# A fused attention and feed-forward kernel: chunks 3 and 4 turned by VectorE, and new lists that set the order of the work

## Chip, cores and metric

One core of a Trainium2 chip runs the whole kernel. The metric is device time in microseconds of one execution, the median of several runs; less is better. The profile is one further execution with the hardware profiler. TensorE's granted clock is at its upper level (2.4 GHz) throughout: the page shows 9 in each of 40 slices, 90% or more of it.

## What is computed

Attention with pooled keys and values for 8 batches and 8 heads (576 queries, head size 64, keys and values averaged over 8 neighbours to 72), then a feed-forward layer with softplus over all 4608 tokens (512 wide, 2048 hidden):

```python
k_p = k.reshape(B, H, Sp, pool, D).mean(axis=3)          # Sp = 72
v_p = v.reshape(B, H, Sp, pool, D).mean(axis=3)
scores = scale * np.matmul(q, k_p.transpose(0, 1, 3, 2))
scores = scores - np.max(scores, axis=-1, keepdims=True)
attn = np.exp(scores)
attn = attn / (np.sum(attn, axis=-1, keepdims=True) + 1e-09)
x = np.matmul(attn, v_p)                                  # to (4608, 512)
h = x @ w_in
g = np.maximum(h, 0.0) + np.log1p(np.exp(-np.abs(h)))
out = g @ w_out
```

All is float32. Large products are made of three products of rounded parts: each operand is split into a rounded value in the type fp32r and a remainder (`x` is both parts of the attention's output, `w` and `l` those of the weights, `gh`/`g` and `gl` those of the softplus).

## The kernel before

The 4608 tokens are cut in 18 chunks of 256 (`CT`), each of two tiles of 128 tokens (`T`). For each chunk come the attention (queries against the 72 pooled keys, exponential, probabilities times values, which gives `x`) and the feed-forward layer (`h` from `x`, `g` from `h`, and the product with the second weight). The program has two parts.

The **first part** holds the feed-forward work of chunks 0 to 2 (`feed`; lines 690 and 715), the attention of chunks 0 to 3 (`attend`), the making of the split weights from the integer halves that are loaded, and the pooling of keys and values. The **steady part** holds the feed-forward work of chunks 3 to 17, in pairs of two pieces of the hidden width (`first_products`, line 743, then `second_products`), each beside the attention of the next chunk. Chunk 3's second products are 24 straightforward ones (`pair2`, line 786); from chunk 4 on (`NF` = 4) a pair is made of seven products of combined operands (line 895). For these VectorE and ScalarE make sums of pieces of `g` (`sf`, `so`: lines 805 to 824), and, once, combinations of weights (`d`, `t`, `w`: lines 848 to 864).

The attention needs its queries and its probabilities with tokens along the free axis. Two ways to turn them exist:

- By TensorE: products with an identity matrix. Queries: `qT`, line 403, names `qTp<-ident,q`. Probabilities of the first 64 keys: `PT`, line 484, `ptp<-ident,pm`. Those of the last 8 keys, in three copies: lines 496 and 610, `ltp<-ident,pe`. ScalarE copies each result out of PSUM. Chunks 0 to 2 do so, chunk 3 (in `attend(N1)`, `N1` = 3, tile by tile) and chunk 4 (`BY_PE = (4,)`).
- By VectorE, chunks 5 to 17: a stream transpose of blocks of 32 by 32 (`turn`, line 524, 128x1024 elements). For queries ScalarE then spreads the blocks by 16 copies (line 535). For probabilities four stores (`leave`, line 528) and one load (`enter`, line 531) on SyncE's queue carry the blocks through memory. The last keys are turned on VectorE too (line 1487), and spread by 12 small copies.

After that come the scores (lines 423 and 557), the smallest negated score and its subtraction (`least`, `less`), one exponential for a chunk, sums and reciprocal, the products `pm` and `pe`, and the product with the values (`avp`, lines 657 and 664); ScalarE rounds it (`x`, line 671) and VectorE makes the remainder (line 674).

What stands in a row on each engine is not the order of the code. Each step is entered as an operation with an engine, a cost, what it comes after, and the buffers (slots) that it uses. A planner (`Order.run`) lays the operations out one after another: of those that could begin first it takes the one of highest rank, which is the length of the longest chain that follows it plus a number `first`. Two tables written by hand, `HASTE` for the first part and `SOONER` for the steady part, add to `first` of single operations by their number. The order found is emitted as it stands, so an engine that reaches an instruction whose input is late stands still with all that is behind it.

## Time and profile before

| what | us |
|---|---|
| median of 3 runs | 862.92 |
| lowest and highest | 862.19 and 863.48 |
| span of the profiled execution | 860.2 |
| TensorE busy | 847.5 (99%) |
| TensorE loading weights | 823.3 (96%) |
| VectorE busy | 666.3 (77%) |
| ScalarE busy | 509.2 (59%) |

The span runs from the first to the last instruction on the core; the device time of the runs also holds what lies around it, and the median is 2.7 us above this span. The page is read from the chain that ended last (which engine sets the end), then by stages, since the engines' shares differ between the first 340 us and the rest, and then by the waits of the engine that the chain names.

### The profile page before, as it was taken

To read this page: it belongs to the slowest core of one execution; us is meant where nothing else is said; L and a number is where in the kernel's file an instruction comes from. 1 tells how busy PE (TensorE), PEld (TensorE's weight loads), DVE (VectorE), ACT (ScalarE), POOL (GpSimd) and SP (SyncE) were. 2 spreads that over 40 slices of the span, in tenths; PEclk is the share of its full clock that TensorE was granted. 3 is DMA by queue.
4 is the path that set the end of the run, shared out by engine and by line. 5 is a ranking of instruction groups with operands and counts; after the bars stand their busy time and mean duration, and the time that the engine had idled before them with its cause. 6 is when DMAs were issued, how large, how long until landed. Compare 5 with 4: busy or idle time off the path is not lost.

```text
span 860.2 us, 21310 instructions
## 1 busy us (share of the span) xinstructions
PE 847.5 (99%) x8520; PEld 823.3 (96%) x8520; DVE 666.3 (77%) x1562; ACT 509.2 (59%) x1138; POOL 3.8 (0%) x33
## 2 busy tenths in 40 slices
PE   8999999999999989999999999999999999999997
PEld 6799999999999989999999999999999999999997
DVE  6899999868887888877788787877777765667554
ACT  5964333446557785857486837574747676454522
POOL 1000000000000000000000000000000000000000
PEclk9999999999999999999999999999999999999999
DMA  8975536455889789778978897678777666667671
GB/s 261 322 226 177 204 139 196 142 178 182 278 304 287 246 277 290 253 247 272 284 244 266 264 288 256 221 247 289 256 259 246 227 230 220 220 229 245 229 247 74
DMA packets 116451, 204.82 MB, mean 238 GB/s; under 512 B 47104, under 2 KB 68096, under 8 KB 116352
## 3 DMA queue, kind: packets, MB, share of 16 engines
q1 hardware_dynamic: 116352, 203.46, 72.3%
q8 instruction: 67, 1.10, 0.5%
q14 instruction: 32, 0.26, 0.1%
HBM read 174.06 MB, written 29.36 MB: 236 GB/s over the span
## 4 chain that ended last, share of the span: by engine, by line
PE 92%; DVE 3%; DMA 2%; ACT 2%; issue 1%; SPq 0%; DVEq 0%; ACTq 0%
PE h L743 37%; PE m L895 30%; PE acc L715 7%; PE h L690 6%; PE acc L786 3%; PE avp L657 2%; PE sc L557 2%; PE avp L664 1%; DMA l<-wi 1%; DMA t<-t 1%; DMA kvst<-in_k_dram 1%; PE kps L1134 1%; ACT qT L535 1%; ACT E L448 0%; PE m L557 0%
## 5 line engine op out<-in xcount | busy, mean ns | idle before, releaser
L743 PE MATMUL h<-x,l 128*128 128x256 f32 x2748 | 333.1, 277 | 0.1
L743 PEld LDWEIGHTS h<-x,l 128*128 128x128 f32 x2748 | 321.8, 188 | 0.7 <-DMA l<-wi 0.3
L751 ACT ACTIVATE g<-h 128x512 f32<-128x512 f32 x120 | 71.9, 599 | 159.7 <-PE h L743 156.5
L895 PE MATMUL m<-w,so 128*128 128x256 f32 x1134 | 149.0, 277 | 1.2 <-ACT so L819 1.0
L895 PEld LDWEIGHTS m<-w,so 128*128 128x128 f32 x1134 | 137.9, 188 | 1.8 <-ACT so L819 1.2
L819 ACT CAST so<-sf 128x512 fp32r<-128x512 f32 x112 | 69.7, 622 | 52.8 <-DVE sf L808 50.0
L805 DVE TENSOR_TENSOR sf<-g 128x128 f32<-128x128 f32 x112 | 32.2, 288 | 85.9 <-ACT g L751 85.5
L824 DVE TENSOR_TENSOR so<-sf,so 128x512 fp32r<-128x512 f32 x112 | 77.1, 688 | 25.7 <-ACT so L819 24.7
L535 ACT COPY qT<-turn 32x256 f32<-32x256 f32 x208 | 84.1, 404 | 12.2 <-DVE turn L524 5.0
L895 PE MATMUL m<-w,gh 128*128 128x256 f32 x476 | 90.4, 278 | 0.0
L772 DVE TENSOR_TENSOR gl<-g,gh 128x384 fp32r<-128x384 f32 (+1 forms) x120 | 67.3, 561 | 7.3 <-ACT gh L765 5.2
L895 PEld LDWEIGHTS m<-w,gh 128*128 128x128 f32 x476 | 71.8, 188 | 0.6
L895 PE MATMUL m<-w,gl 128*128 128x256 f32 x238 | 65.9, 277 | 0.0
L695 ACT ACTIVATE g<-h 128x256 fp32r<-128x256 f32 x96 | 32.1, 383 | 55.3 <-PE h L690 32.4
L765 ACT ACTIVATE gh<-h 128x384 fp32r<-128x384 f32 (+1 forms) x120 | 59.2, 493 | 0.2 <-DVE gl L772 0.2
L690 PE MATMUL h<-x,w 128*128 128x256 f32 x396 | 49.9, 278 | 0.1
L690 PEld LDWEIGHTS h<-x,w 128*128 128x128 f32 x396 | 47.1, 188 | 0.6 <-ACT g L695 0.3
L715 PE MATMUL acc<-w,g 128*128 128x256 f32 x264 | 47.0, 279 | 0.0
L895 PEld LDWEIGHTS m<-w,gl 128*128 128x128 f32 x238 | 44.7, 188 | 0.0
L916 DVE TENSOR_TENSOR o<-o,m 128x256 f32<-128x256 f32 x98 | 39.8, 418 | 3.3 <-ACT o L908 0.4
L715 PEld LDWEIGHTS acc<-w,g 128*128 128x128 f32 x264 | 39.9, 188 | 0.1
L895 PE MATMUL m<-l,gh 128*128 128x256 f32 x196 | 37.4, 279 | 0.0
(214 smaller groups left out, 1333.3 us busy)
## 6 DMA issues: line engine op xcount, KB each, us to landing
l<-wi SPq DMA_DIRECT2D x224, 512.0 KB
out_dram<-o SPq DMA_DIRECT2D x36, 256.0 KB
q<-in_q_dram SPq DMA_DIRECT2D x32, 256.0 KB
kst<-in_k_dram SPq DMA_DIRECT2D x24, 288.0 KB
moved_p<-turn SPq DMA_DIRECT2D x52, 128.0 KB
pT<-moved_p SPq DMA_DIRECT2D x13, 512.0 KB
vst<-in_v_dram SPq DMA_DIRECT2D x24, 256.0 KB
stage<-in_moe_w_in_dram SPq DMA_DIRECT2D x22, 256.0 KB
```

The costliest lines, as they stand in the source:

```text
L535: nc.scalar.copy(out=o, in_=x[a * B32:(a + 1) * B32, s].rearrange("p (u m i) -> p u m i", u=T, i=B32))
L690: nc.tensor.matmul(out=ps[:, 0:CT], lhsT=row(w, kc), rhs=x[:, kc], start=first and kc == j == 0, stop=last and kc == KC - 1 and j == 2)
L715: nc.tensor.matmul(out=accs[c][t][:, ns], lhsT=a[:, ts], rhs=w[:, ns], start=f == 0 and n == j == 0, stop=f == FC - 1 and n == 1 and j == ...
L743: nc.tensor.matmul(out=ps[:, k * CT:(k + 1) * CT], lhsT=row(w, kc), rhs=x_[c][i][:, kc], start=first and n == 0, stop=last and n == len(or ...
L751: nc.scalar.activation(out=g, in_=x.rearrange("p (b i) -> p b i", i=P), func=AF.Softplus)
L765: nc.scalar.activation(out=gh, in_=quarters(c, x.rearrange("p (b i) -> p b i", i=P)), func=AF.Softplus)
L772: nc.vector.tensor_tensor(out=gl, in0=quarters(c, g), in1=gh.bitcast(F32), op=ALU.subtract)
L805: tt(out=sf[:, 2], in0=g[:, 0], in1=g[:, 2], op=ALU.add)
L819: nc.scalar.copy(out=so[:, 0], in_=ss[c, u])
L824: nc.vector.tensor_tensor(out=so[:, 1], in0=sf, in1=so[:, 0].bitcast(F32), op=ALU.subtract)
L895: nc.tensor.matmul(out=ms[c][n], lhsT=x, rhs=y, start=u == 0 and j == 0 and n in (1, 6, 5, 4), stop=u == FP - 1 and j == 2 and n in (2, 7, ...
L916: nc.vector.tensor_tensor(out=o, in0=in0, in1=m[n], op=how)
```

## The change

Chunks 3 and 4 are turned by VectorE as chunks 5 to 17 are. One function, `turned_attention`, makes the attention of chunks 3 to 17; for chunk 3 (`early`) it is called in the first part, and `attend` is left with chunks 0 to 2. TensorE's transposes of chunks 3 and 4 go: 16 products `qTp`, 16 `ptp` and 6 `ltp`. VectorE gets two turns of 128x1024 and one of 128x128 for each of the two chunks, ScalarE 28 small copies for each, and SyncE's queue four stores and one load of probabilities for each.

The planner of the first part gets what that of the steady part had: a transfer is an operation that holds the queue for a time, and one that holds a resource `TRANSFER` and lands 1.85 us after. Costs of operations are smaller by what is now a lag between engines (0.13 to 0.2 us), and two neighbours on VectorE of which one needs the other get a lag of 0.1 us. `HASTE` and `SOONER` are new throughout. With `short`, the last product of a chunk's last keys is cut in two where the chunk holds queries of two batches, so that the one at the end has 64 columns.

```diff
-                        + [x.end + (x.lag if x.engine != o.engine or x.lag > 1 else 0)
+                        + [x.end + (x.lag if x.engine != o.engine or x.lag > 1 else self.same.get(o.engine, 0))
...
-    BY_PE = (4,)
...
+        i, t = sp[-1]
+        short = [*sp[:-1], (i, slice(t.start, t.stop - D)), (i, slice(t.stop - D, t.stop))]
         for r, ps in enumerate(pss):
             for g in range(2):
-                for i, t in sp:
+                for i, t in short if len(sp) > 1 and r == g == 1 and sp[-1][1].start < CT - D else sp:
                     nc.tensor.matmul(out=ps[:, g * CT + t.start:g * CT + t.stop],
...
+    TRANSFER, LANDING, nothing = "transfer", 1.85, lambda: None
+    LAGS = {PE: 0.2, ACT: 0.14, DVE: 0.13, TRANSFER: LANDING}
+    todo.begin, todo.table = {SYNC: 0.8, TRANSFER: 0}, "exp"
+    todo.in_turn, todo.same = (TRANSFER,), {DVE: 0.1}
+
+    def op(engine, cost, fn, after=(), slots=(), **more):
+
+        if engine is not SYNC:
+            return todo.op(engine, cost, fn, after, slots, LAGS[engine], **more)
+        queue, work = cost
+        o = todo.op(SYNC, queue, fn, after, slots, 0, **more)
+        return todo.op(TRANSFER, work, nothing, [o], slots, LANDING, first=more.get("first", 0))
...
-        return 0.14 + 0.00094 * n
+        return 0.03 + 0.0009 * n
 
     def dve1(n):
-        return 0.14 + 0.00054 * n
+        return 0.06 + 0.00053 * n
...
-                if c < N1:
...
-                    def less(x=x, i=i, s=s):
-                        if c not in e_:
-                            new_E(c)
-                        x.less(i, s.tile)
-                    ends.append(op(DVE, 0.46, less, [d, *e_free], [s, s_mn]))
...
-        if c == N1:
-            ex = op(ACT, 1.2, lambda: exponential(e_[c]), subs, table="exp")
         for x, ends, s_E, s_sm, s_pm, s_pe in norms:
-            if c == N1:
-                ends = [op(DVE, 0.75, lambda x=x, n=s_sm: x.sum(n.name), [ex], [s_sm])]
...
+    def turned_attention(c):
+        early = c == N1
+        here = lambda kind: [] if early else [Slot(kind)]
+        soon = lambda run: {} if early else dict(first=EARLY, home=run)
+        s_q, s_E, s_lt = here("q"), here("E"), Slot("lt_")
+        tiles = [Tile(c, t) for t in range(T)]
+
+        def load():
+            load_q(c)
+        o_q = op(SYNC, (1.1, 2.0), load, [q_free[c - 1, i] for i in range(T)] if early else qT_done.get(c - 1, ()), s_q)
+        subs = []
+        qT_done[c], score_done[c], av_done[c], x_done[c] = [], [], [], []
+        sp, s_mn, x_q = spans(c * CT, (c + 1) * CT), Slot("mn"), []
+        s_t, turns, s_qT = Slot("ld"), {}, [Slot("qT") for _ in range(T if early else 1)]
+
+        def turn_q():
+            turns["q"] = one.tile([P, A, T * HP * B32], F32, tag=s_t.name, name="turn")
+            turn(turns["q"], qt_[c].rearrange("p t h d -> p (t h d)"))
+
+        def spread_q(a, pair):
+            for s in pair:
+                across(q_place(slice(0, T))[s * B32:(s + 1) * B32, :, :, a * B32:(a + 1) * B32],
+                       turns["q"], a, s)
+        for x in tiles:
+            x.q = q_place(x.t)
+        o = op(DVE, 1.17, turn_q, [o_q, *entered["q"]], [*s_q, s_t])
+        qT_done[c].append(o)
+        for a in range(A):
+            for pair in ((0, 1), (2, 3)):
+                x_q.append(op(ACT, 0.83, lambda a=a, pair=pair: spread_q(a, pair), [o], [s_t, *s_qT]))
+        entered["q"] = x_q
+        old = c - 2 if c - 2 >= NF else None
+        ss = [Slot("bank"), Slot("bank"),
+              Slot("bank") if early else Slot("acc") if old is None else banks_of[old][3]]
+
+        def third_bank():
+            return bank(ss[2], "sc") if old is None else ms[old]["rest"]
+        p = op(PE, 1.4, lambda: pair_scores(
+            c, tiles, [*(bank(s, "sc") for s in ss[:2]), (third_bank(), old is None)]),
+               [*x_q, *parts_of(sp, k_done if early else k_ready), m_begun.get(old), *([av[c - 1]] if early else [])],
+               [*s_qT, *ss], **soon("m"))
+        score_done[c].append(p)
+        for j in (2, 0, 1):
+            ps = lambda j=j: third_bank() if j == 2 else ss[j].tile
+            o = op(DVE, 0.22 if j == 2 else 0.6,
+                   lambda j=j, ps=ps: pair_least(c, j, ps(), s_mn.name), [p], [ss[j], s_mn],
+                   first=HURRY if j == 2 else 0)
+            for part in range(1 if j == 2 else 3):
+                subs.append(op(DVE, 0.22 if j == 2 else (0.37, 0.21, 0.14)[part],
+                               lambda j=j, ps=ps, part=part: pair_less(c, j, part, ps()),
+                               [o, *(e_free if early else ())],
+                               [ss[j], s_mn, *s_E], first=HURRY if j == 2 else 0))
+        return lambda where: probabilities(c, s_E, s_lt, subs, where)
...
+    def probabilities(c, s_E, s_lt, subs, where):
+
+        early = c == N1
+        soon = lambda run: {} if early else dict(first=EARLY, home=run)
+        s_pT, s_pe, x, s_sm, s_pm, s_t = Slot("pT"), Slot("pe"), {}, Slot("sm"), Slot("ld"), Slot("ld")
+        if early:
+            ex = op(ACT, 1.1, lambda: exponential(e_[c]), subs, table="exp")
+        else:
+            ex = op(ACT, 1.1 + TABLE, lambda: exponential(e_[c]), [*subs, where], s_E)
+            op(ACT, TABLE, lambda: None, [ex], first=5000)
+
...
+        o = op(DVE, 1.28, sums_p, [ex], [*s_E, s_sm])
+        o = op(DVE, 0.4, reciprocals, [o], [s_sm])
+        m = op(DVE, 1.14, main_p, [o], [*s_E, s_sm, s_pm], first=FIRST)
+        e = op(DVE, 0.2, ends_p, [o], [*s_E, s_sm, s_pe])
+        o = op(DVE, 1.17, turn_p, [m], [s_pm, s_t], first=FIRST)
+        ways = [op(SYNC, (0.5, 0.36), lambda a=a: leave(x["turn"], "p", a), [o, *entered["p"]], [s_t], first=FIRST)
+                for a in range(A)]
+        entered["p"] = [op(SYNC, (0.35, 2.1), enter_p, ways, [s_pT], first=FIRST)]
+        lows = [*entered["p"], *last_keys(c, [o, e], lambda: x["pm"], s_pm, s_pe, s_lt)]
+        sp = spans(c * CT, (c + 1) * CT)
+        ss = [Slot("bank"), Slot("bank")]
+        o = op(PE, 1.7 if len(sp) == 1 else 2.1, lambda: av_products(c, [bank(s, "avp") for s in ss]),
+               [*lows, *parts_of(sp, v_done if early else v_ready), *([x_free[0]] if early else [])],
+               [*ss, s_lt, s_pT], **soon("h"))
+        av_done[c].append(o)
+        s_x = [] if early else [Slot("x")]
+        if s_x:
+            x_slot[c] = s_x[0]
+        for r, s in enumerate(ss):
...
-    attend(N1)
+    turned_attention(N1)(None)
...
-    HASTE = {27: -130, 29: -3, 34: -120, 36: -120, 45: 40, 46: 20, 48: -180, 55: -2, 56: -10, 57:
...
+    HASTE = {2: 5889, 4: 7020, 6: 5020, 8: 1140, 10: 1278, 13: -860, 20: 170, 29: 3721, 31: 3711, 33: 3265, 39:
...
-    with tc.manual_schedule(engines={ACT, DVE, PE, SYNC}):
-        for o in todo.run():
-            o.fn()
+        todo.ops[i].first += x
+    ctx.enter_context(tc.manual_schedule(engines={ACT, DVE, PE, SYNC}))
+    for o in todo.run():
+        o.fn()
...
-        if c in BY_PE:
-            s_qT, s_qb = [Slot("qT")], [Slot("bank") for _ in tiles]
-
-            def transposes():
-                for x, s in zip(tiles, s_qb):
-                    x.qT(bank(s, "qTp"))
-            o = op(PE, 0.97, transposes, [o_q, *av_done.get(c - 1, ())], [s_q, *s_qb], first=EARLY, home="m")
-            qT_done[c].append(o)
-            for x, s, n in zip(tiles, s_qb, Q):
-                x_q.append(op(ACT, act(512), lambda x=x, s=s, n=n: x.qT_out(s.tile, n), [o], [s, *s_qT]))
-        else:
-            s_t, turns, s_qT = Slot("ld"), {}, [Slot("qT")]
...
-        if c in BY_PE:
-            for x in tiles:
-                s_sm, s_pm = Slot("sm"), Slot("G")
-                o = op(DVE, 0.785, lambda x=x, n=s_sm: x.sum(n.name), [ex], [s_E, s_sm])
-                o = op(DVE, 0.44, x.reciprocal, [o], [s_sm])
-                m = op(DVE, 0.72, lambda x=x, s=s_pm: x.main(s.name), [o], [s_E, s_sm, s_pm])
-                es.append(op(DVE, 0.255, lambda x=x, s=s_pe: pair_ends(c, x, s.name), [o], [s_E, s_sm, s_pe]))
-                s = Slot("bank")
-                o = op(PE, 0.55, lambda x=x, s=s: x.PT(bank(s, "ptp")), [m], [s, s_pm], first=EARLY, home="h")
-                lows.append(op(ACT, act(512), lambda x=x, s=s: x.PT_out(s.tile), [o], [s, s_pT]))
-        else:
...
-        if c in BY_PE:
-            s_l = Slot("bank")
-            p = op(PE, 0.27, lambda: pair_last(c, bank(s_l, "ltp")), es, [s_l, s_pe], first=EARLY, home="m")
-            for a in range(2):
-                h = op(ACT, act(256), lambda a=a: pair_high(c, a, s_l.tile, a), [p], [s_l, s_lt])
-                lows.append(op(DVE, dve2(256), lambda a=a: pair_low_ends(c, a, s_l.tile), [h], [s_l, s_lt]))
-            for a in range(2):
-                lows.append(op(ACT, act(256), lambda a=a: pair_high(c, a, s_l.tile, 2), [p], [s_l, s_lt]))
-        else:
-            lows += last_keys(c, [o, *es], lambda: x["pm"], s_pm, s_pe, s_lt)
...
-                    rest = steady_attention(c + 1)
+                    rest = turned_attention(c + 1)
...
-    SOONER = {37: -100.0, 43: -300.0, 44: -100.0, 48: -700.0, 49: -900.0, 53: -50.0, 58: -400.0, 59: -400.0,
...
+    SOONER = {17: 1346, 18: 2216, 28: 99, 36: -84, 44: -1517, 50: -21, 51: 527, 69: -2053, 77: -29, 83: -13.8,
```

On TensorE, at the start of the steady part: the end of a row of chunk 3's h products (`h<-x,w`), then chunk 4's queries turned, then chunk 3's second products (`acc<-w,gh` and `acc<-w,gl`). Before:

```order
L743 MATMUL h<-x,w 128x256 x24
L403 MATMUL qTp<-ident,q 128x128 x8
L786 MATMUL acc<-w,gh 128x256 x2
L786 MATMUL acc<-w,gl 128x256
L786 MATMUL acc<-w,gh 128x256 x2
L786 MATMUL acc<-w,gl 128x256
L786 MATMUL acc<-w,gh 128x256 x2
```

After, the same place:

```order
L744 MATMUL h<-x,w 128x256 x24
L787 MATMUL acc<-w,gh 128x256 x2
L787 MATMUL acc<-w,gl 128x256
L787 MATMUL acc<-w,gh 128x256 x2
L787 MATMUL acc<-w,gl 128x256
L787 MATMUL acc<-w,gh 128x256 x2
```

The eight transposes are gone; h and the second products are neighbours.

On TensorE, at the seam of the two parts: chunk 3's product with the values (`avp`), chunk 2's products (`h<-x,l`, `acc<-l,g`), and the first of chunk 3's h (`h<-x,w` at line 743). Before:

```order
L715 MATMUL acc<-l,gl 128x256
L657 MATMUL avp<-pT,vs_102 64x256 x8
L664 MATMUL avp<-lt__1039,vlo_104 128x256 x4
L690 MATMUL h<-x,l 128x256 x48
L715 MATMUL acc<-l,g 128x256 x2
L743 MATMUL h<-x,w 128x256 x17
L715 MATMUL acc<-l,gl 128x256
```

After:

```order
L691 MATMUL h<-x,l 128x256 x12
L656 MATMUL avp<-pT,vs_102 64x256 x8
L665 MATMUL avp<-lt__2440,vlo_104 128x256 x4
L716 MATMUL acc<-l,g 128x256 x2
L716 MATMUL acc<-l,gl 128x256
L716 MATMUL acc<-l,g 128x256 x2
L716 MATMUL acc<-l,gl 128x256
L716 MATMUL acc<-l,g 128x256 x2
L716 MATMUL acc<-l,gl 128x256
L716 MATMUL acc<-l,g 128x256 x2
L716 MATMUL acc<-l,gl 128x256
L744 MATMUL h<-x,w 128x256 x24
```

In the rows before, 48 products of chunk 2 and two more stand between `avp` and chunk 3's h; in those after, twelve do. Chunk 3's scores (`sc`), which stood in one row before some 51 us into the span and a second one later, now stand as one row late in the first part, with 168 products of 256 columns and a small transpose from there to `avp`:

```order
L716 MATMUL acc<-l,g 128x256 x2
L716 MATMUL acc<-l,gl 128x256
L691 MATMUL h<-x,l 128x256 x12
L556 MATMUL sc<-kT_100,qT 64x72 x32
L691 MATMUL h<-x,l 128x256 x12
```

On VectorE, in chunk 4's first combined products: sums of `g` (`sf`, `so`), weights' combinations (`t`, `w`), and the probabilities of the next chunk (`sm`, `pm`). Before:

```order
L805 TENSOR_TENSOR sf<-g 128x128
L806 TENSOR_TENSOR sf<-g 128x128
L807 TENSOR_TENSOR sf<-sf,g 128x128
L808 TENSOR_TENSOR sf<-g,sf 128x128
L772 TENSOR_TENSOR gl<-g,gh 128x384
L864 TENSOR_TENSOR t<-d,t 128x2x256
L824 TENSOR_TENSOR so<-sf,so 128x512
L864 TENSOR_TENSOR w<-d,w 128x2x256 x2
L1529 TENSOR_REDUCE sm<-E 128x16
L1533 TENSOR_SCALAR sm<-sm 128x16
L1534 RECIPROCAL sm<-sm 128x16
```

After, from the same sums on:

```order
L806 TENSOR_TENSOR sf<-g 128x128
L807 TENSOR_TENSOR sf<-g 128x128
L808 TENSOR_TENSOR sf<-sf,g 128x128
L809 TENSOR_TENSOR sf<-g,sf 128x128
L523 STREAM_TRANSPOSE turn<-q 128x8x4x32
L825 TENSOR_TENSOR so<-sf,so 128x512
L253 TENSOR_TENSOR vst<-vst 128x2x256
L253 TENSOR_TENSOR vst<-vst 128x2x128
L253 TENSOR_TENSOR vp<-vst 128x128
L1381 TENSOR_REDUCE sm<-E 128x16
L1385 TENSOR_SCALAR sm<-sm 128x16
L1386 RECIPROCAL sm<-sm 128x16
```

The turn of a chunk's queries and the pooling of values (`vst`, `vp`) stand where the weights' combinations stood. Behind them, where before a second set of sums, `pm` and a turn of probabilities followed, the pooling of keys (`kst`, `kp`) now stands as well:

```order
L809 TENSOR_TENSOR sf<-g,sf 128x128
L773 TENSOR_TENSOR gl<-g,gh 128x384
L825 TENSOR_TENSOR so<-sf,so 128x512
L253 TENSOR_TENSOR kst<-kst 72x2x256
L253 TENSOR_TENSOR kst<-kst 72x2x128
L253 TENSOR_TENSOR kp<-kst 72x128
L773 TENSOR_TENSOR gl<-g,gh 128x384
L523 STREAM_TRANSPOSE turn<-pm 128x8x4x32
```

## Rows read from the trace of the kernel before

**Rows 1.** The page, busy time by engine, and the last chain by engine:

```profile
PE 847.5 (99%) x8520; PEld 823.3 (96%) x8520; DVE 666.3 (77%) x1562; ACT 509.2 (59%) x1138; POOL 3.8 (0%) x33
...
PE 92%; DVE 3%; DMA 2%; ACT 2%; issue 1%; SPq 0%; DVEq 0%; ACTq 0%
```

**Rows 2.** Windows: us; busy us (instructions) PE, PEld, DVE, ACT, POOL; clock; DMA:

```profile
60.00:80.00 20.00, 19.85 (x173) 19.59 (x172) 19.43 (x36) 9.33 (x23) 0.00 (x0) 1.00 0.41 136
160.00:245.00 85.00, 84.45 (x869) 82.91 (x868) 68.83 (x153) 44.86 (x92) 0.21 (x2) 1.00 0.65 213
340.00:600.00 260.00, 259.93 (x2657) 255.14 (x2651) 203.63 (x517) 173.13 (x368) 0.63 (x6) 1.00 0.81 263
600.00:855.00 255.00, 255.00 (x2529) 251.69 (x2528) 167.86 (x434) 141.52 (x294) 0.42 (x4) 1.00 0.67 226
```

**Rows 3.** Waits of TensorE: line, releaser: us in total, times, longest:

```profile
PE acc L715 <- DVE gl L701: 1.0, 2, 0.5
PE m L895 <- ACT so L819: 1.0, 1, 1.0
PE m L557 <- ACT qT L535: 0.9, 1, 0.9
PE avp L657 <- DVE E L595: 0.8, 1, 0.8
...
PE m L895 <- DVE so L824: 0.2, 1, 0.2
```

**Rows 4.** Timeline of TensorE, chunk 4's queries: start, us, instruction:

```profile
185.50 2.88 PE L743 MATMUL h<-x,w 128*128 128x256 f32 x24
188.23 1.04 PE L403 MATMUL qTp<-ident,q 128*128 128x128 f32 x8
189.02 0.48 PE L786 MATMUL acc<-w,gh 128*128 128x256 f32 x2
189.34 0.28 PE L786 MATMUL acc<-w,gl 128*128 128x256 f32 x1
```

**Rows 5.** Timeline of TensorE, chunk 3's probabilities, chunk 4's last keys:

```profile
62.75 0.63 PE L484 MATMUL ptp<-ident,pm 128*128 128x128 f32 x4
63.13 0.48 PE L715 MATMUL acc<-w,g 128*128 128x256 f32 x2
63.46 0.28 PE L715 MATMUL acc<-w,gl 128*128 128x256 f32 x1
...
215.91 0.38 PE L610 MATMUL ltp<-ident,pe 128*64 128x128 f32 x2
216.04 1.17 PE L743 MATMUL h<-x,l 128*128 128x256 f32 x8
```

**Rows 6.** Groups of VectorE by shape: busy us, mean ns | idle before:

```profile
L772 DVE TENSOR_TENSOR gl<-g,gh 128x384 fp32r<-128x384 f32 x112 | 61.8, 552 | 3.0 <-ACT gh L765 3.0
...
L674 DVE TENSOR_TENSOR x<-avp,x 128x512 fp32r<-128x512 f32 x36 | 23.7, 684 | 3.7 <-ACT x L671 3.6
...
L253 DVE TENSOR_TENSOR kst<-kst 72x512 f32<-72x512 f32 x24 | 16.3, 680 | 0.3 <-DMA kst<-in_k_dram 0.3
...
L524 DVE STREAM_TRANSPOSE turn<-q 128x1024 f32<-128x1024 f32 x13 | 16.1, 1237 | 0.0
```

**Rows 7.** Groups of ScalarE by shape, the rounding of x:

```profile
L671 ACT CAST x<-avp 128x512 fp32r<-128x512 f32 x36 | 19.8, 589 | 8.9 <-PE avp L664 8.8
```

**Rows 8.** Waits of VectorE, 160 to 245 us:

```profile
DVE vst L253 <- DMA vst<-in_v_dram: 2.3, 1, 2.3
```

**Rows 9.** Timeline, two turned chunks: scores and turn; turn, reading back, product:

```profile
339.78 1.07 PE L557 MATMUL sc<-kT,qT 64*64 64x72 f32 x53
...
351.98 1.25 DVE L524 STREAM_TRANSPOSE turn<-pm 128x1024 f32<-128x1024 f32 x1
...
486.16 1.25 DVE L524 STREAM_TRANSPOSE turn<-pm 128x1024 f32<-128x1024 f32 x1 [0.65 <-ACT qT L535]
...
491.56 0.32 SPq L531 DMA_DIRECT2D pT<-moved_p  x1
...
499.04 1.09 PE L657 MATMUL avp<-pT,vs 64*64 64x256 f32 x16
```

More of the change, by code (lines that the diff above doesn't have):

```diff
@@ L1191, in attend @@
             ends, ss = [], [Slot("bank"), Slot("bank")]
-            p = op(PE, 0.7, lambda x=x, ss=ss: x.scores([bank(s, "sc") for s in ss]), [o, *keys],
+            p = op(PE, 0.72, lambda x=x, ss=ss: x.scores([bank(s, "sc") for s in ss]), [o, *keys],
                    [s_qT, *ss])
@@ new lines, in pooled_attention_softplus_ffn @@
+    todo.last = Op(None, 0, None, (), (), 0, -1)
+    s_w, x_w = Slot("bank"), []
+    o = op(DVE, 0.3, lambda: x_w.append(ones()), first=2000)
+    op(PE, 3.6, lambda: warm(x_w[0], bank(s_w, "warm"), (512, 384)), [o], [s_w], first=2000)
+    batch(0)
+    batch(1)
+    for f in range(FC):
+        weights(f)
+    for c in range(N1):
+        attend(c)
+    for c in range(N1 - 1):
+        feed(c)
+    todo.first = 1000
+    turned_attention(N1)(None)
+    todo.first = 0
+    feed(N1 - 1)
+    keys_values(2, score_done[N1 - 1], [av[N1 - 1]])
@@ new lines, in pooled_attention_softplus_ffn @@
+    other = [b for b in BANKS if b not in acc_banks]
+    kinds = {"h": other[:2], "acc": other[2:4], "bank": other[4:], "ld": LD, "q": "a", "pT": "a", "qT": "a", "lt_": "a",
+             "pe": "a", "mn": "ab", "sm": "ab", "E": "a", "kp": "a", "vp": "a", "S": "ab", "x": "b",
+             **{y.kind: {"a": "b", "b": "a"}[y.name] for y in last_g},
+             "G": [f"G{i}" for i in range(4)] + O}
+    ends = {e: max(o.end for o in todo.ops if o.engine == e) for e in (ACT, DVE, PE, SYNC, TRANSFER)}
```

372 lines of the change are left out of this document (139 added, 233 removed), and 83 rows, old and new, of tables (HASTE, SOONER).

## The prediction

> **What bounds the kernel now.** I read the page's busy times and its chain first: TensorE is busy for 847.5 us of an 860.2 us span, and 92% of the chain that ended last is TensorE's [rows 1]. So the end moves with what TensorE has to do and with the moments at which it stands idle; nothing that VectorE or ScalarE saves counts by itself. The windows say where that can change: from 340 us to 855 us TensorE is busy for 514.9 of 515 us and VectorE for 371 [rows 2]; nothing there waits, so nothing there can be won by a better order. In 60 to 80 us the picture is another: VectorE is busy for 19.43 of 20 us beside TensorE's 19.85, so the two run in lockstep, and work added to VectorE there is felt at once. In 160 to 245 us VectorE has 16.2 of 85 us free [rows 2], though part of that is waiting: 2.3 us of it is one load of values [rows 8]. The list of TensorE's waits gives the idle time that can vanish: 0.5 us at the first part's end (one of the two waits for gl), then 1.0, 0.2, 0.9 and 0.8 us in the 300 to 322 us stretch, 3.4 us in all [rows 3]. The other 0.5 us for gl lies at 43.8 us, in front of any change, and I let it stand.
>
> The profiled execution spans 860.2 us and the median is 862.9; I take the 2.7 us between them as fixed and make the sum on the median.
>
> **TensorE work that goes.** A product of 256 columns has a pitch of 2.73 us / 24 = 0.1135 us (from the start of the 24 to the start of what follows, 185.50 to 188.23) [rows 4]. The eight transposes of chunk 4's queries take 0.79 us from start to start (188.23 to 189.02), and the products behind them begin late: two take 0.32 us to the next start (189.02 to 189.34) where 0.23 would do, so 0.09 us belongs to the change of kind. That is 0.88 us. Chunk 4's eight transposes of probabilities are the same instruction on the same shape: 0.88 again. Its last keys' two take 0.13 us (215.91 to 216.04) [rows 5] and 0.09 to leave: 0.22. Chunk 4: 2.0 us. Chunk 3 has the same eight for queries, 0.88; its probabilities come as two groups of four at 0.38 (62.75 to 63.13) and, by the same reading of the next rows (63.13 to 63.46, 0.33 where 0.23 would do), 0.10 to leave: 0.96 for both [rows 5]; its last keys two groups at 0.24, counted as chunk 4's with a little more to enter: 0.48. Its scores come in one go in place of two, one change of kind fewer: 0.2. Chunk 3: 2.5 us. **Together 4.5 us**, all of it on the path since TensorE does not wait around it. The bound from below is 4.0 (without the changes of kind that two neighbours could share), from above 5.
>
> The split of the last keys' final product adds one instruction in four chunks at the same number of columns. The trace has no such pair at that place; it has products of fewer columns that follow one another without a gap, so I count 0, bounds -0.1 and +0.2 us in each, and take 0 because what is streamed stays the same.
>
> **TensorE idle time that goes.** The new lists and costs move instructions; the five waits above stand next to chunks 3 to 6, whose order is made anew. Some like them can come back. I let the 3.4 us vanish and price the new waits on their own.
>
> **The seam between the parts.** On TensorE chunk 3's scores move from about 51 us to late in the first part, and its values' product now has 12 products behind it before its own h (before: 48 and more). Two waits can arise. First, h needs x: ScalarE's rounding of the second half is 0.59 us [rows 7] and VectorE's remainder 0.68 [rows 6], with the hand-overs some 1.7 us, while 12 products cover 12 x 0.1135 = 1.36: 0.4 us, bounds 0 and 1. Second, chunk 3's probabilities now travel through memory. Between its scores and its values' product stand 168 products of 256 columns and a small transpose, 19.4 us. The chain needs, by chunks that already do this: from the end of the scores (339.78 + 1.07 = 340.85) to the start of the turn (351.98) 11.1 us, the turn 1.25, from its end to the end of the issue that reads the moved probabilities back 4.5 (487.41 to 491.88) [rows 9], together 16.9 us; then that transfer has to land. The row of the product itself starts 11.6 us after the turn's end (499.04), but TensorE came to it without waiting, so it is an upper bound: 11.1 + 1.25 + 11.6 = 24. The wait is thus between 0 and 4.6 us. I take 0.6, close to the lower end: 2.5 us are left for the landing of half a megabyte, and the 11.1 us held planned slack. **Seam: +1.0 us**, bounds 0 and 5.6.
>
> **VectorE in the first steady products.** This is where the turning of chunks 4 and 5 is paid. Between the second and the fourth of chunk 4's combined products VectorE's row gains a turn of queries, 1.24 us, a gl of 0.55, and the pooling of one piece of k and one of v, whose first addition is 0.68 [rows 6] and whose two further ones are of half and a quarter of that size, an estimate of 1.4 us each; and it loses three subtractions of 512 columns, the size of the same 0.68 row, 2.05 us. Net 1.24 + 0.55 + 2.8 - 2.05 = 2.5 us in two of TensorE's rounds. TensorE comes there 4.5 us sooner, and what VectorE must have done by then has not become less. Cover: VectorE's free 16.2 us between 160 and 245 us; if all of them can be filled, this costs 0, and if none can, it costs 2.5 here and as much again for the two turns of chunk 3 that lie before it, 5.0. **I take 2.5.** ScalarE gets some 7 us of copies more in each of the two chunks, and was busy for 44.9 of the same 85 us [rows 2]; I count 0 and would look there next if VectorE is not it. SyncE gets two sets of four stores and one load of half a megabyte; nothing waits on it in that stretch save the load of values above: 0, bound 1.
>
> The Trainium skill has a rule that speaks against this change: in "VectorE: DVE Perf Modes", section "Rules for kernel authors", a transpose of 128 by 128 belongs on TensorE where a PSUM destination will do. This kernel's turning by VectorE gives blocks of 32 only, and the copies and the trip through memory are the price of that. By the trace the rule is right on effort (0.88 us of TensorE against a 1.24 us turn, sixteen copies and a transfer) and misses which engine is full; it would decide if VectorE became the bound, the last rival below.
>
> **Sum:** 862.9 - 4.5 - 3.4 + 1.0 + 2.5 = 858.5 us (a span of 855.8). From 50 us back, at the start, the order of the first loads changes, with the same bytes; I count 0, bounds -2 and +2.
>
> **Rivals.**
> 1. No new wait at all. The lists are planned with separate times for a transfer's occupancy and its landing, so the seam and the burst may fit: 862.9 - 7.9 = 855.0, and 853 if the start is better by 2. Against it: VectorE's lockstep in 60 to 80 us.
> 2. VectorE sets the pace up to 245 us: the slower side. In 60 to 80 us VectorE has under 3% free [rows 2], and what turns chunk 3 is added behind that. If its free time in 160 to 245 us is bound to what it waits for (loads, ScalarE), TensorE's 4.5 us are lost there, VectorE's 5.0 us come straight through, and the seam takes 3.3, the middle between 1.0 and its bound of 5.6: TensorE stands 8.3 us later than before at 245 us, and the 2.9 us of waits after 300 us are won all the same: 862.9 + 8.3 - 2.9 = 868. It decides from the point at which what is lost exceeds 4.5 + 3.4 = 7.9 us; below that the result is not slower. Against it: the net added work is a third of the free 16.2 us.
> 3. Partly so: VectorE or the moved probabilities give back what the transposes saved: the losses are 6.2 to 9.6 us, and the time within 861.2 to 864.6.
> 4. Turning is no gain for a chunk at all: the two chunks' turns come onto the path whole, 2 x 2.5 us, and no wait is won: 862.9 - 4.5 + 5.0 = 863.4, inside rival 3's range and 0.03 of its chance. This is what the Trainium skill's rule above would make of it. Against it: thirteen chunks are turned already, and TensorE has no wait from 340 us on [rows 2].
> That the change does not do what it says is excluded by the instruction rows: chunks 3 and 4 have no transposes on TensorE any more.
>
> **How the numbers follow.** The forecast, with new waits of 0 to 6.2 us, covers 855.0 to 861.2: chance 0.60. Below 855.0 (rival 1 with a better start): 0.12. Rival 3: 0.14. Rival 2: 0.14. About 0.2% (1.7 us) is what a measurement of this kernel can tell from no change, so faster means below 861.2: 0.72; same 0.14; slower, above 864.6: 0.14. The range leaves out about one in ten at each side at most: 853.5 to 864.5.
>
> **What would show it.** In the profile after: TensorE's busy time falls by 4 to 5 us; groups of qTp, ptp and ltp shrink to those of chunks 0 to 2; in the list of TensorE's waits the five waits are gone, and a wait of avp or h at about 175 us and of m for so or gl at 240 to 260 us take their place, of 3 to 4 us together. VectorE's busy time in 160 to 245 us rises from 68.8 to 72 or more. From 330 us on nothing waits. I am wrong if TensorE waits for VectorE in many small pieces between 60 and 160 us (rival 2), or if it waits anew in the first 50 us for a load, or if the waits around 300 us stay.

## The result, and the profile after

The changed kernel takes 871.53 us (median of 4 runs, 868.19 to 872.38); the kernel before, on the same chip, 863.2 us (862.19 to 864.21). The ratio is 1.0086, with an interval of 1.0061 to 1.0111: slower by 0.9%, where 0.5% faster was forecast. The profiled execution spans 869.6 us (860.2 before).

The page after, busy time by engine and the last chain by engine; it answers to [rows 1]:

```profile
PE 850.6 (98%) x8486; PEld 826.9 (95%) x8486; DVE 666.7 (77%) x1556; ACT 521.4 (60%) x1184; POOL 3.9 (0%) x34
...
PE 81%; ACT 7%; DVE 5%; DMA 4%; issue 1%; SPq 1%; DVEq 0%; ACTq 0%
```

TensorE has 34 recorded instructions fewer and is busy 3.1 us longer. Its share of the chain falls from 92% to 81%: other engines and transfers now release it more often.

The same four windows as [rows 2] (us; busy us and instructions of PE, PEld, DVE, ACT, POOL; clock; DMA share; GB/s):

```profile
60.00:80.00 20.00, 20.00 (x172) 20.00 (x172) 18.86 (x24) 7.78 (x18) 0.00 (x0) 1.00 0.73 241
160.00:245.00 85.00, 80.83 (x810) 78.89 (x809) 68.37 (x144) 56.06 (x124) 0.21 (x2) 0.96 0.63 201
340.00:600.00 260.00, 256.96 (x2527) 251.63 (x2519) 197.22 (x499) 165.06 (x349) 0.42 (x4) 1.00 0.81 261
600.00:855.00 255.00, 254.91 (x2577) 251.28 (x2576) 172.87 (x448) 147.04 (x309) 0.52 (x5) 1.00 0.70 234
```

From 160 to 245 us TensorE stands 4.2 us where it stood 0.55, and the mean clock there is 0.96. From 340 to 600 us, where nothing waited, 3.0 us are missing. VectorE's busy time in 160 to 245 us did not rise (68.8 before); ScalarE's did, from 44.9 to 56.1.

TensorE's waits by line, which answer to [rows 3] (us in total, times, longest):

```profile
PE m L896 <- DVE gl L773: 3.3, 5, 1.5
PE avp L656 <- DVE d L854: 2.2, 1, 2.2
PE acc L716 <- DVE gl L702: 1.6, 1, 1.6
...
PE m L556 <- ACT qT L534: 1.3, 1, 1.3
...
PE m L896 <- ACT gh L766: 0.5, 1, 0.5
```

Adding up TensorE's waits behind 150 us in the timeline gives 9.3 us; the same sum before is 3.5. One releaser in this list misleads: for `avp` it names VectorE's `d`, long done, where the next section finds a transfer.

**Where the 9 us come from.** The last product starts at 855.1 us before and at 864.1 after. Instruction by instruction on TensorE: transposes, scores and changes of kind that went, -4.3; more waits, +5.9; products at half clock, +3.4; and a different pitch of unhindered products (the time from one start to the next), +3.4. The first 44 us make -0.2 and small gaps the rest, some 0.8. The next three paragraphs show the three losses.

**The moved probabilities land late.** Chunk 4's probabilities travel through memory now. VectorE ends their turn at 215.66 us:

```profile
214.41 1.25 DVE L523 STREAM_TRANSPOSE turn<-pm 128x1024 f32<-128x1024 f32 x1 [0.19 <-ACT qT L534]
```

SyncE's queue from there (start, us, instruction):

```profile
215.69 1.77 SPq L527 DMA_DIRECT2D moved_p<-turn  x4
217.88 0.93 SPq L876 DMA_DIRECT2D w<-t  x2
219.70 1.35 SPq L301 DMA_DIRECT2D vst<-in_v_dram  x2
221.10 0.59 SPq L530 DMA_DIRECT2D pT<-moved_p  x1
```

TensorE's rows at the product with the values:

```profile
224.78 1.07 PE L744 MATMUL h<-x,l 128*128 128x256 f32 x8
228.04 1.78 PE L656 MATMUL avp<-pT,vs 64*64 64x128 f32 x32 [2.19 <-DVE d L854]
```

Two loads of `w` and the two of `vst` stand between the stores and the load that reads them back; the product begins 12.4 us after the turn's end and TensorE stood 2.2 us for it. Before, chunk 4's probabilities were turned on TensorE and took no such way.

**Behind that wait the clock is at its lower level.** Windows of 2 us, columns as above:

```profile
226.00:228.00 2.00, 0.00 (x0) 0.00 (x0) 1.90 (x6) 1.39 (x3) 0.00 (x0) 1.00 0.95 385
228.00:230.00 2.00, 1.96 (x33) 1.66 (x34) 1.66 (x3) 0.62 (x1) 0.00 (x0) 0.64 0.95 291
230.00:232.00 2.00, 2.00 (x10) 2.00 (x11) 0.48 (x1) 0.67 (x2) 0.00 (x0) 0.50 0.97 352
232.00:234.00 2.00, 2.00 (x11) 2.00 (x11) 1.64 (x4) 1.02 (x2) 0.00 (x0) 0.50 0.98 301
234.00:236.00 2.00, 2.00 (x13) 2.00 (x13) 1.93 (x5) 0.00 (x0) 0.00 (x0) 0.65 0.79 297
```

After one empty window TensorE is granted 0.50, which is 1.2 of 2.4 GHz, and starts 10 or 11 products in 2 us instead of 19 or 20; from 236 us on it shows 1.00 again. What the four windows with less than 1.00 lack is 2 x (0.36 + 0.50 + 0.50 + 0.35) = 3.4 us. The page's row of 40 slices shows it as one 8 among the 9s. These 3.4 us are the profiled run's, whose mean granted clock was 0.995. The other three runs had 0.998, 0.998 and 0.999, so at most a part of this loss, and two of them took 871.39 and 872.38 us all the same; what those lost in its place no trace shows.

**Engines stand behind buffers that the stores still read.** ScalarE and VectorE in two places (start, us, instruction, in brackets the wait ahead of it):

```profile
173.84 0.62 ACT L861 CAST t<-d 128x512 fp32r<-128x512 f32 x1 [2.53 <-DMA moved_p<-turn]
...
541.95 1.25 DVE L523 STREAM_TRANSPOSE turn<-q 128x1024 f32<-128x1024 f32 x1 [2.85 <-DMA moved_p<-turn]
```

Each is an instruction that TensorE doesn't need soon; but it writes a buffer that the four stores of a turn still read, and what TensorE does need stands behind it on the same engine. A third row names the same releaser, and there it misleads (VectorE, then ScalarE):

```profile
449.63 0.31 DVE L594 TENSOR_TENSOR E<-m,mn 128x144 f32<-128x144 f32 x1 [1.64 <-PE m L896]
449.86 0.30 DVE L1346 STREAM_TRANSPOSE pm<-pe 128x128 f32<-128x128 f32 x1
...
450.20 0.50 ACT L1352 CAST pm<-pm 128x128 fp32r<-128x128 f32 x2 [2.36 <-DMA moved_p<-turn]
```

This cast rounds the last keys, which VectorE turned up to 450.16 us, and in the kernel it writes the buffer of `pm`, which the stores don't read. At 537.97 us the same cast starts as closely behind the same turn, and there the trace names the turn. So ScalarE waited here for VectorE, which had stood 1.64 us for one of TensorE's products. TensorE's rows that follow the three:

```profile
175.58 0.39 PE L716 MATMUL acc<-l,gl 128*128 128x256 f32 x1 [1.63 <-DVE gl L702]
...
452.86 0.50 PE L896 MATMUL m<-w,gh 128*128 128x256 f32 x2 [0.54 <-ACT gh L766]
...
544.62 0.39 PE L896 MATMUL m<-w,gl 128*128 128x256 f32 x1 [1.47 <-DVE gl L773]
```

**The pitch.** Windows of before, then of after, on TensorE alone (us; busy and instructions; clock; DMA share; GB/s), in a stretch where nothing waits:

```profile
92.00:112.00 20.00, 20.00 (x179) 1.00 0.46 157
120.00:140.00 20.00, 20.00 (x179) 1.00 0.57 185
```

```profile
92.00:112.00 20.00, 20.00 (x173) 1.00 0.40 140
120.00:140.00 20.00, 20.00 (x172) 1.00 0.65 212
```

Same products, clock 1.00, no gaps, and 172 or 173 where there were 179. Single starts in the records stand 113.3 ns apart before and 117.8 after. In after one train (products that follow one another without a break) of some 920, from 48 to 157 us, runs at the longer pitch, 4.1 us in all. Before has slower trains too, but shorter ones, the longest of 292 products from 236 to 271 us; the difference over the whole run is 3.4 us.

### The profile page after: what moved, and what is told of

Same layout as the page of the kernel before. It is cut to its first block, busy times and chain, and to the rows that moved or that the text cites. A ratio compares the mean times of both kernels' runs of the same rounds, so it can differ in the third digit from the quotient of the medians.

```text
span 869.6 us, 21311 instructions
## 1 busy us (share of the span) xinstructions
PE 850.6 (98%) x8486; PEld 826.9 (95%) x8486; DVE 666.7 (77%) x1556; ACT 521.4 (60%) x1184; POOL 3.9 (0%) x34
## 4 chain that ended last, share of the span: by engine, by line
PE 81%; ACT 7%; DVE 5%; DMA 4%; issue 1%; SPq 1%; DVEq 0%; ACTq 0%
PE h L744 33%; PE m L896 28%; PE h L691 7%; PE acc L716 7%; ACT qT L534 2%; PE avp L656 2%; PE avp L665 2%; PE sc L556 2%; PE acc L787 1%; DMA moved_p<-turn 1%; DMA q<-in_q_dram 1%; DVE turn L523 1%; DMA kvst<-in_k_dram 1%; ACT L752 1%; ACT g L752 1%
## 5 line engine op out<-in xcount | busy, mean ns | idle before, releaser
L534 ACT COPY qT<-turn 32x256 f32<-32x256 f32 x240 | 96.8, 403 | 8.1 <-PE sc L556 2.4
```

Source lines behind the costliest of these rows:

```text
L534: nc.scalar.copy(out=o, in_=x[a * B32:(a + 1) * B32, s].rearrange("p (u m i) -> p u m i", u=T, i=B32))
```

## Experiments

Each ran beside the kernel before on the same chip: 863.45 us for e1 to e4, 863.49 for e5 to e8, 862.83 for e9 to e11.

**The changed kernel again**, with no edit.

> The changed kernel unaltered, for a second profile. In the first one TensorE stood still for 1.8 us at 174 us, 2.4 us at 226 us (with a granted clock of 0.50 for 6.7 us behind it) and eight shorter times, and its 256-column products had a pitch of 118 ns in place of 113 from 48 to 158 us and from 545 to 597 us. If the waits belong to the order of the instructions, they stand at the same places, within 0.3 us each. If the two pitches belong to the order too, the same stretches are slow; if they are a chance of the execution, the slow stretches lie elsewhere and the time differs from 871.5 by up to 4 us.

874.06 us, ratio 1.0111 (1.0082 to 1.0139). The largest waits stand at the same places, not all of the same length (2.17 us at 545 us, where the first profile had 1.47), and the long train has the longer pitch again. The product with chunk 4's values, now with the transfer named as its releaser, and the window behind it:

```profile
229.57 1.25 PE L656 MATMUL avp<-pT,vs 64*64 64x128 f32 x32 [1.49 <-DMA pT<-moved_p]
...
230.00:232.00 2.00, 2.00 (x41) 1.83 (x33) 1.85 (x4) 1.17 (x3) 0.00 (x0) 1.00 1.05 324
```

Here TensorE kept 1.00. But behind the 2.17 us at 545 us it was granted 0.50 from 545.9 to 549.3 us, where the first profile had 1.00. So these waits and the long train's pitch belong to the program; where the half clock comes differs from one execution to the next, and so does the pitch of other trains: the products from 240 to 259 us stood 117.8 ns apart here and 113.3 in the first profile. The long train began 2.0 us later than there, behind waits of 2.01 us at 10.9 us for VectorE and 1.25 us at 24.9 us for a load of keys.

**Before, with the transposes of chunks 3 and 4 made twice.**

```diff
-            for m in range(HP):
+            for m in [*range(HP)] * (2 if self.c in (3, 4) else 1):
```

(and so at lines 483 and 495; chunk 4's two transposes of last keys, line 610, stay single, so that 36 are added, not the 38 of the expectation)

> The kernel before, with each transpose of chunks 3 and 4 on TensorE issued twice (38 more instructions, same result). If the price of a transpose in the prediction is right (8 in 0.79 us, the change of kind paid once), it is 3.4 us slower, 0.4%. If TensorE's time there is hidden behind VectorE's, it is slower by under 1 us. If removing these products cannot have gained what was predicted, this run shows it.

869.81 us, ratio 1.0055 (1.0032 to 1.0077). Sixteen transposes of queries take 1.67 us to the next start, where eight took 0.79 [rows 4]:

```profile
193.85 1.91 PE L403 MATMUL qTp<-ident,q 128*128 128x128 f32 x16
195.52 0.48 PE L786 MATMUL acc<-w,gh 128*128 128x256 f32 x2
```

That is 0.88 for eight more, without a further change of kind. The prediction had 0.88 as well, but made of 0.79 and 0.09 for the change of kind. All doubled groups make 3.9 us. The rest of the loss in the profile is mostly pitch: this kernel's windows of 92:112 and 120:140 hold 172 products each, so a train of 838 products that ran at 113 ns before runs at 118, 3.8 us, and VectorE's first turn comes only at 210 us.

**After, with the load that reads the probabilities back ahead of four others.** On SyncE's queue, the order against that of after:

```diff
 L527 DMA moved_p<-turn 32x4x256 x4
+L530 DMA pT<-moved_p 128x1024
+L301 DMA vst<-in_v_dram 64x2x512 x2
 L876 DMA w<-t_1_119 128x2x256
 L876 DMA w<-t_1_119 128x512
-L301 DMA vst<-in_v_dram 64x2x512 x2
-L530 DMA pT<-moved_p 128x1024
```

> The changed kernel, with two loads (one of weight combinations, one of values) moved on SyncE's queue from ahead of to behind the load that brings chunk 4's probabilities back; nothing else moves. Theory of the trip through memory: the load is no longer queued behind 1 MB, TensorE's wait of 2.2 us at 226 us goes, and with it the 6.7 us at half clock (3.3 us): 866 us. Rival, VectorE late by a whole us: the wait shrinks by under 0.5 us and the time stays at 871. If the clock fell for another reason than the wait, the wait goes and the low clock stays: 869.

868.51 us, ratio 1.0061 (1.0041 to 1.008). In the profiled run the wait and the half clock are gone (another of its nine runs had a mean granted clock of 0.994); a later load is late in their place:

```profile
226.09 1.10 PE L656 MATMUL avp<-pT,vs 64*64 64x128 f32 x32
...
232.50 2.62 PE L744 MATMUL h<-x,l 128*128 128x256 f32 x20 [0.82 <-DMA l<-wi]
```

In the profiles the last product starts 3.2 us earlier than after's (860.8 against 864.1). This confirms that the trip and what stood in it made the wait. It did not come from an earlier issue. Wait of SyncE's queue, then its row:

```profile
SPq L530 <- DMA moved_p<-turn: 3.5, 1, 3.5
...
221.73 0.34 SPq L530 DMA_DIRECT2D pT<-moved_p  x1
```

The read now waits 3.5 us for the four stores to land, and its issue ends 6.1 us after the turn's end (215.97 to 222.07), against 6.0 in after. What became shorter is the rest: at most 4.0 us from there to the product, where after took 6.3 with four transfers ahead of the read.

**After, with one cast and one subtraction of the weights' combinations (`t<-d`, `t<-d,t`) behind chunk 2's `g` and `gl`.**

```diff
-    for o in todo.run():
+    for o in rearranged(todo.run(), [(737, 'after', 690), (738, 'after', 691)]):
```

(`rearranged` moves numbered operations within their engine's row)

> The changed kernel, with two steps that round a weight combination (one on ScalarE, one on VectorE) moved behind chunk 2's softplus and its remainder; the first of them waited 2.5 us for the stores of chunk 3's probabilities to land, since it writes the buffer that they read. Theory of the trip: TensorE's wait of 1.6 us for gl at 174 us goes: 1.5 us faster. Rival, VectorE sets the pace: the wait stays above 1 us, and the time within 0.5.

870.53 us, ratio 1.0074 (1.0047 to 1.01). The wait of 1.63 us at 175.6 us is gone, and a part of it turns up 8 us on, at the other wait that the prediction named for the seam:

```profile
183.66 3.01 PE L744 MATMUL h<-x,w 128*128 128x256 f32 x24 [1.04 <-DVE x L675]
```

There it was 0.35 us. The wait for chunk 4's probabilities (2.17) and the half clock stayed.

**After, with the last keys' final product in pieces of 64 columns everywhere, and after without `short`.**

```diff
-        short = [*sp[:-1], (i, slice(t.start, t.stop - D)), (i, slice(t.stop - D, t.stop))]
+        short = [*sp[:-1], *((i, slice(a, a + D)) for a in range(t.start, t.stop, D))]
```

```diff
-                for i, t in short if len(sp) > 1 and r == g == 1 and sp[-1][1].start < CT - D else sp:
+                for i, t in sp:
```

> The changed kernel, with the last product of chunks 2, 4, 11 and 13's last keys cut in pieces of 64 columns throughout (in place of 128 and 64 for chunks 2 and 11). Theory of the two pitches: a train of 256-column products keeps the pitch it was entered with; the train of 923 products behind chunk 2 runs at 118 ns in three profiles of three since it is entered behind a 128- and a 64-column product, those entered behind 64-column products alone run at 113. Then the stretch from 48 to 158 us runs at 113, and that behind chunk 11 at about 550 us too: 5.5 us less, 866. Rival, the pitch is set by what else runs (VectorE at 95%, transfers): the stretch stays at 118 ns and the time at 871.

> The changed kernel without the cut of the last keys' last product (four products fewer); the one part of the change that can be undone alone. Theory of the two pitches: the trains behind chunks 4 and 13 run at 118 ns again, as before the change, some 200 products and 1 us slower; the one behind chunk 2 stays at 118. Rival, the cut costs its four instructions: 0.2 us faster, not to be told from nothing.

872.28 us (ratio 1.0098, 1.0075 to 1.012) and 870.40 (1.0065, 1.0042 to 1.0089). In both the windows of 92:112 and 120:140 hold 172 or 173 products, as after. The columns with which a chunk ends do not set the pitch of the long train, and `short` is worth nothing that these runs can tell.

**After with the two moves above (the trip's somewhat further back), and more:** `gl` ahead of the turns and last keys that stood in front of it, ScalarE's last keys behind `gh` or copies that are needed first, chunk 2's last 12 products ahead of chunk 3's `h`; the pieces of 64 columns too.

> The changed kernel with its waits taken away by order alone, and the cut of e5: the loads of e3 (the load of weights now also ahead), the two steps of e4, chunk 2's last 12 products moved ahead of chunk 3's h, five steps of VectorE and five of ScalarE moved by one to three places so that the remainders gl, which TensorE waits for, stand ahead of turns and of the spreading of last keys. No instruction is added or left out but the cut. Theory, the loss is in the waits, the clock behind one of them, and the pitch: waits of 11 us fall to 3, the half clock goes, the long train runs at 113: 857 us, faster than the kernel before by 6. Rival, VectorE sets the pace: waits come back elsewhere and it stays above 866.

867.35 us, ratio 1.0044 (1.0026 to 1.0063). In the profiled run the waits behind 150 us fall from 9.3 to 5.4 us, and no window shows a lower clock; other runs of the twelve had a mean granted clock down to 0.994. The largest that is left:

```profile
PE avp L656 <- DVE E L594: 1.8, 3, 1.0
```

The long train keeps 118 ns, and the 857 us that were expected did not come. The order of the work thus explains about half of the loss: 4.2 us by the medians, and 4.9 and 3.1 beside the two kernels above.

**After, with both lists empty.**

```diff
-    HASTE = {2: 5889, 4: 7020, 6: 5020, ...
+    HASTE = {}
...
-    SOONER = {17: 1346, 18: 2216, 28: 99, ...
+    SOONER = {}
```

> The changed kernel with both tables of numbers empty, so that its order comes from the planner's rank alone. If the tables carry the order that hides the transfers, the time is above 880. If the tables are what makes the new waits, it is below 871.

900.28 us, ratio 1.0404 (1.0376 to 1.0432). Its largest waits of TensorE:

```profile
PE avp L656 <- DMA pT<-moved_p: 12.0, 2, 10.9
PE h L744 <- DMA l<-wi: 7.6, 6, 2.3
```

What the planner's costs alone arrange is 3% worse than the lists; and its largest wait is again for the moved probabilities. TensorE was granted 0.50 in five stretches, 30.7 us together, so a part of the loss is the clock.

**A break in the long train**, in after (e9), in the kernel of e7 (e10), and six of them in the kernel of e7 (e11, `(2, 1), (2, 2), (2, 4), (0, 5), (0, 8), (2, 8)`): two transposes into a bank that the next products overwrite.

```diff
         hi, lo = wi[f]
+        if (c, f) in ((2, 1),):
+            for m in range(2):
+                nc.tensor.transpose(out=ps[:, m * P:(m + 1) * P], in_=ident, identity=ident)
         for kc in rows:
```

> The changed kernel with one break in its long train of 256-column products: two 128x128 transposes of the identity go into the bank of chunk 2's second first-half block (about 57 us) ahead of the twelve products that overwrite it. Theory A (a train keeps the pitch with which it was entered, and a re-entry behind another kind of product draws it anew, mostly at 113 ns as in the kernel before): the products from 57 to 158 us stand 113 ns apart instead of 118, about 830 x 4.5 ns = 3.7 us less, for 0.3 us of transposes; the end comes 3.4 us earlier, 868.1 beside 871.5 to 874. Theory B (the pitch belongs to the stretch, to what VectorE, the queues and the memory do beside it): the products stay at 118 ns and the time grows by 0.3. The waits at 174, 226, 307, 452 and 537 to 543 us and the half clock behind 226 stay in both.

> The same break put into the kernel of e7_all, whose waits are about half as long. Theory A: pitch 113 ns from 57 to 164 us, 3.4 us earlier than e7_all's 867.35, so 864, within 0.2 per cent of the kernel before. Theory B: 867.5.

> The kernel of e7_all with the same two transposes ahead of six first-half blocks of chunks 0 and 2 between 57 and 140 us: six re-entries instead of one. Theory A with a pitch that is drawn anew at each: some of the seven pieces at 113 and some at 118 ns, each constant in itself, at a cost of 1.7 us for the transposes; the sum between 864 and 869. Theory A with a cause in the transposes themselves: all pieces at 113, 865. Theory B: all at 118, 869.

868.79 us (ratio 1.0065, 1.0041 to 1.0089), 867.46 (1.0036, 1.0014 to 1.0059) and 867.68 (1.0051, 1.0032 to 1.007). The windows 60:88, 92:112 and 120:140 of e9, of e10 and of e11 (after has 240, 173, 172):

```profile
60.00:88.00 28.00, 28.00 (x249) 1.00 0.82 261
92.00:112.00 20.00, 20.00 (x172) 1.00 0.35 131
120.00:140.00 20.00, 20.00 (x173) 1.00 0.64 197
```

```profile
60.00:88.00 28.00, 28.00 (x250) 1.00 0.77 253
92.00:112.00 20.00, 20.00 (x179) 1.00 0.36 134
120.00:140.00 20.00, 20.00 (x172) 1.00 0.63 196
```

```profile
60.00:88.00 28.00, 28.00 (x249) 1.00 0.77 245
92.00:112.00 20.00, 20.00 (x179) 1.00 0.42 156
120.00:140.00 20.00, 20.00 (x179) 1.00 0.68 218
```

A re-entry does change the pitch, at once and with VectorE, queues and memory as busy as before: theory B falls. Theory A holds in part: the pitch of e9 fell back to 118 at 90 us and that of e10 at 115 us with no break that the records show (one product's record is missing at each place), so a train need not keep the pitch with which it was entered. In e11 every piece behind a break ran at 113, up to 155 us; whether the transposes themselves bring it is not shown. The time hardly follows. In e11 the longer pitch costs 1.7 us in all where e7 had 6.5, yet its waits behind 150 us are 7.7 us instead of 5.4 and its time is e7's: TensorE came sooner and waited 2.13 us at 243.8 us for a `gl`, where e7 waited 0.52. In e10 that wait was 2.73 us, with half clock behind it. By the medians no kernel beats the one before; e10 and e7 come nearest.

## Why the prediction was wrong, by its own steps

**TensorE work that goes: right.** 4.5 us forecast, 4.3 measured: 1.58 for `qTp`, 1.50 for `ptp`, 0.41 for `ltp`, 0.34 of entries, 0.43 of scores, inside the stated bound. e2 measures the unit from the other side, 0.88 for eight transposes; that the sum agrees although its parts (0.79 and 0.09) don't is luck.

**Idle time that goes: four of five.** The waits at 302 to 322 us went, 2.9 us; the one for `gl` at the first part's end grew from 0.55 to 1.63. The wait of 0.91 for spread queries was chunk 7's; chunk 6's scores have one of the same kind now, 1.29 us, counted below.

**The seam: the size within its bounds, the cause missed.** 1.0 us forecast, bounds 0 to 5.6; 1.63 + 0.35 = 2.0 measured. The 0.35 is the 0.4 put down for `x`. The 0.6 for late probabilities of chunk 3 was zero: its product began at 179.78 us without a wait. The 1.63 is a buffer, above, and e4 shows it: with the cast moved it goes, and shifts part of itself to `x`.

**VectorE in the first steady products: 2.5 us forecast, 2.1 found** (0.24, 1.29 and 0.60 us between 255 and 310 us). But the 1.29 are ScalarE's copies of queries, which stand behind last keys that it spreads and behind a stand of 1.26 us at 270.66 us, where it writes a buffer that a store of `t` still reads. ScalarE was counted at 0 on its share of busy time; with the 0.54 us at 452.9 us it cost 1.8 us, and its stand for a buffer at 173.84 led to the 1.63.

**The step that failed first is the term for SyncE, "0, bound 1": chunk 4's trip through memory.** The prediction put SyncE's two sets of four stores and one load at nothing because nothing waits on that queue in the trace of before, where chunk 4 makes no such trip; the moved probabilities it priced at the seam alone, for chunk 3. Chunk 4's move in the same way, beside loads that took 0.95 of the transfer engines' time, and cost 2.2 us and, in the profiled run, 3.4 us of half clock. The estimate of the trip was too low as well: 4.5 us from the turn's end to the end of the issue that reads back became 6.0 (215.66 to 221.69), and in e3, with nothing else in the queue between, 6.1; the landing took another 6.3 where 2.5 were held likely. The 11.6 us that [rows 9] showed for another chunk were called an upper bound; they bound that chunk only, and chunk 4 needed 12.4. In e3 and e7, where no other transfer stands ahead of the read, the product began 10.1 and 10.7 us after the turn's end and did not wait.

**The second is the sentence that nothing waits from 330 us on.** It took an order for granted that the change makes anew everywhere. 0.54, 0.31, 0.72 and 1.47 us of waits stand between 452 and 545 us, the last behind stores that still read a buffer, 0.72 behind a turn put ahead of `gl`, the first two behind last keys that ScalarE got late from VectorE. SyncE, at 0 with a bound of 1, is where the 1.63 and the 1.47 begin: not its queue's time, but how long a store holds what it reads. That the five old waits vanish and new ones cost 3.5 us came out as 3.5 us of waits before and 9.3 after.

**The third could not be read from the profile of before alone: the pitch**, 3.4 us. [rows 4] gave 113.5 ns for one train, and it was taken for all. That there are two pitches stood in the trace of before (the 292 products from 236 to 271 us), in no row that the prediction used; which trains of the new order would get the longer one did not.

The sum with measured terms is -4.3 + 5.9 + 3.4 + 3.4 - 0.2 = 8.2 us beside 9.0 in the profile. The medians give 8.3; that this agrees so well is partly luck, since the half clock is the profiled run's.

**The rivals.** The time lies beyond rival 2's 868, but its mechanism did not act: between 60 and 160 us no wait for VectorE appeared, and VectorE's busy time in 160 to 245 us stayed at 68.4 instead of rising to 72. Rival 4 has the better sign and the wrong mechanism: the turns did not come onto the path whole; what costs is the trip through memory and what stands behind it, and the pitch. The Trainium skill's rule beside it is that a 128 by 128 transpose belongs on TensorE ("VectorE: DVE Perf Modes", "Rules for kernel authors"). The measured time agrees with it in sign, 0.9% slower with the turns on VectorE; but the lists changed with them. The chance for slower, 0.14, was probably too small because each trip and each list was priced where a wait was expected, and not everywhere.

**What stays open.** How the loss divides between the turns and the new lists, since the only run that parts them, e8, has no lists at all; why a train enters at one pitch or the other; why the clock fell behind some stands and not others; what the runs lost that had no half clock; and what of e7's remaining 3.9 us against before is pitch (2.7 us in its profile) and what is waits, since a shorter pitch in e11 came back as waits.

## What to carry to other kernels

Price every trip through memory that a change adds, each at its own place, with what stands ahead of its read in the queue, and add what comes behind: the engines that wait for the buffer it reads, and the clock after a stand. Where a change brings new hand-made lists, the whole order is new, and the waits of the old order say little about what the new one leaves. And count starts in a long window before blaming waits: 172 instead of 179 in 20 us is a loss that no wait shows.

## What the runs showed of the hardware

- **Two pitches at a full clock.** Products of 256 columns follow one another every 113.3 or every 117.8 ns, constant over hundreds of them, under the same clock of 1.00. Two small transposes in the train were each time followed by the shorter one (e9, e10, e11); the longer one came back in e9 and e10 at places where the records show no other instruction.
- **Half clock behind some short stands.** In after, e4, e9 and e10 TensorE stood for 2.2, 2.2, 1.2 and 2.7 us between 225 and 244 us and then ran at 0.50 for some 3 to 7 us; in e1, e5, e6 and e11 it stood there for 1.5, 1.8, 1.2 and 2.1 and kept 1.00. Near 545 to 550 us it ran at 0.50 for 3.4 us behind 2.2, 2.3 and 1.8 us in e1, e9 and e11, and kept 1.00 behind 1.5 and 2.0 in after and e5. The length of the stand alone does not decide. The two windows of e10, then those of e11, from the stand on (columns as for e9):

```profile
242.00:244.00 2.00, 0.27 (x2) 1.00 0.96 326
244.00:246.00 2.00, 2.00 (x12) 0.52 1.05 414
```

```profile
242.00:244.00 2.00, 0.24 (x2) 1.00 1.05 401
244.00:246.00 2.00, 2.00 (x19) 1.00 1.00 387
```

- **A turn's way through memory** (four stores of 128 KB, one load of 512 KB) took 12.4 us from the turn's end to the product where four other transfers stood ahead of the read. In e3, e7, e10 and e11, where none did, the product began 10.0 to 10.7 us after it without a wait, so that is an upper bound. The read cannot be issued before the stores have landed: in e3 the queue stood 3.5 us for them, and the transfer engines' share was 0.01 from 220 to 222 us.
